# Rows scattered by expert during the attention, and one body per expert picked by its number of tokens

## The chip, the cores and the metric

One core of one Trainium2 chip. The time is the device time in microseconds of one execution, the median of the runs shown. The engines are named as in the profile: PE is TensorE (PEld its weight loads), DVE is VectorE, ACT is ScalarE, POOL is GpSimd, SP is SyncE. A "q" after an engine's name means its sequencer, the part that loads registers, waits for semaphores and branches. [...]

## What is computed

Chunked attention over 4 batches, 8 heads and 768 positions of 64 values, with 8 memory positions; its output, read as 3072 tokens of 512 values, goes through a mixture of 8 experts. Each token goes to one expert only:

```python
logits = x @ w_gate                      # 3072 x 512 by 512 x 8
expert_idx = np.argmax(logits, axis=1)
gate_w = softmax(logits)[own expert]
h = np.maximum(x_sorted[lo:hi] @ w1[e], 0.0)     # 512 x 1024
y_sorted[lo:hi] = h @ w2[e]                      # 1024 x 512
out = gate_w[:, None] * y                        # back in token order
```

All of it is fp32. The inputs are made with a fixed seed; worked through the reference, they give the 8 experts 529, 195, 426, 381, 565, 320, 162 and 494 tokens.

## The kernel before

`ordinary` does all the work; `general`, behind a test at the end (L890, L891), is a slower form for extreme inputs and is skipped here.

Attention. The loop at L726 goes over 32 blocks of 96 queries, and the order of the instructions is the order in which they are written. In iteration i it loads later blocks on SP's queue, transposes q of block i+2 (`turn_q`), computes `scores(i)` (L593, exponentials on ACT at L606), the values of heads 0 to 3 of block i-1 (`values`, L619, normalised on DVE at L622 and L623), transposes the rows of block i-2 (`turn_xb`, L633), the values of heads 4 to 7 of block i-1, transposes k of block i+3 (`turn_k`) and computes the gate's `logits(i-3)` (L645). These logits go into the last columns of the PSUM bank that `values(i-1, 1)` has filled, so they come after the DVE has read that bank (L623). The rows of a block, x, go to `x_dram` in token order by one DMA from POOL's queue (L626). After each batch of 8 blocks `route` picks the expert of each token and its place among that expert's tokens, in steps that the loop runs one by one; POOL adds up the counts per expert (`seen`, L678), PE turns them into ranks (`rk`, L680 and L681), and DVE writes for each block a 96 x 128 matrix `row_of` (L697).

Between the stages (L767 to L806) the counts are rounded up to tiles of 128 tokens, an expert is found for each of NS = 31 tiles, and a matrix product over the 32 blocks (L798, 64 matmul instructions) gives for each slot of each tile its token and its gate.

Experts. Each of the 31 tiles (L874) loads the w1 and w2 of its expert (2 MB each, SP, L815 and L817, two tiles ahead, address from a register), gathers its 128 rows from `x_dram` by an indirect DMA on POOL (L819), transposes them (`turn_xs`, L830, copied by DVE), computes the first layer (L842: 32 products of 128 x 128 by 128 x 128, each two matmul instructions, so 64), the second (L859: 8 products of 128 x 128 by 128 x 512, so 16 instructions), multiplies by the gate on ACT (L861) and scatters the rows to the output by an indirect DMA on POOL (L862).

Of the kernel before, what the change touches and what calls it, by code (L numbers as in the profile page):

```python
# [67 lines left out]
NV, NQ = 6, 4  # L68

# [25 lines left out]
def _consts():  # L95
# [4 lines left out]
    c["iota"] = np.broadcast_to(p, (128, 128))  # L100
    c["slot"] = np.broadcast_to(128 * np.arange(NS), (128, NS))
# [385 lines left out]
def ordinary(ctx, tc, q, k, v, mem_k, mem_v, moe_w_gate, moe_w1, moe_w2, out, good):  # L487
# [22 lines left out]
    x_dram = dpool.tile([N, DM], F32, name="x_dram")  # L510
# [6 lines left out]
    def const(name):  # L517
# [3 lines left out]
    ident, tri, iota, slot0, rev, token, mask = (  # L521
        const(n) for n in ("ident", "tri", "iota", "slot", "rev", "token", "mask")
# [19 lines left out]
    gate = cpool.tile([QB, NB], F32, name="gate")  # L542
    tile0 = cpool.tile([QB, NB], F32, name="tile0")
    row_of = cpool.tile([QB, NB, 128], F32, name="row_of")
# [65 lines left out]
    def values(i, g):  # L610
        s = st[i]
        if g == 0:
            s["x"] = apool.tile([QB, H, D], F32, name="x", bufs=3)

        bank = ps_o.tile([QB, 512], F32, tag="o", name="o")
# [7 lines left out]
        nc.vector.tensor_tensor(s["x"][:, 4 * g : 4 * g + 4], o[:, :, 0:D], bc(inv, 2, D), op=OP.mult)  # L623
        if g == 1:
            s["x"] = s["x"].rearrange("p h d -> p (h d)")
            nc.gpsimd.dma_start(x_dram[QB * i : QB * i + QB], s["x"])  # L626
        return bank[:, 4 * (D + 1) :]

# [10 lines left out]
    def logits(i, room):  # L639
# [3 lines left out]
        ps = room[:, 0:E]  # L643
        for c in range(DM // 128):
            mm(ps, lhsT=s["xT"][:, c], rhs=wg[:, c], start=c == 0, stop=c == DM // 128 - 1)  # L645
        nc.vector.tensor_copy(lgs[b][:, t], ps)


    def small(shape, name, dt=F32):
        return rpool.tile(shape, dt, name=name)  # L650

    def route(b):
# [17 lines left out]
        yield 1  # L670
        total = small([QB, NQB], "total")
        nc.vector.reduce_sum(total, l, axis=AX_X)
        nc.vector.tensor_scalar(total, total, 1e-9, None, op0=OP.add)
        nc.vector.reciprocal(gate[:, sl], total)
        yield 1

        for t in range(t0, t0 + NQB):
            nc.gpsimd.tensor_tensor(seen[:, t + 1], seen[:, t], onehot[:, t], op=OP.add)  # L678
# [3 lines left out]
        yield 1  # L682
        own = small([QB, NQB, E], "own")
        nc.vector.tensor_tensor(own, rk, oh, op=OP.mult)
        rank = small([QB, NQB], "rank")
        nc.vector.reduce_sum(rank, own, axis=AX_X)
        yield 1
        ri = small([QB, 3, NQB], "ri", I32)
        nc.vector.tensor_copy(ri[:, 0], rank)
        nc.vector.tensor_scalar(ri[:, 1], ri[:, 0], 127, None, op0=OP.bitwise_and)  # L690
        nc.vector.tensor_scalar(ri[:, 2], ri[:, 0], 0x1F80, None, op0=OP.bitwise_and)
        nc.vector.tensor_copy(tile0[:, sl], ri[:, 2])
        low = small([QB, NQB], "low")
        nc.vector.tensor_copy(low, ri[:, 1])
        yield 1
        for t in range(NQB):
            nc.vector.tensor_scalar(  # L697
                row_of[:, t0 + t], iota[0:QB], low[:, t : t + 1], None, op0=OP.is_equal
            )
            if t % 3 == 2:  # L700
                yield 1

# [11 lines left out]
    with tc.manual_schedule():  # L714
        for i in range(3):
            load_k(i)
            load_q(i)
            if i < 2:
                load_v(i)
# [6 lines left out]
        for i in range(NB + 3):  # L726
# [4 lines left out]
            need(i, scores)  # L731
            if 0 <= i - 1 < NB:
                values(i - 1, 0)
            need(i - 2, turn_xb)
            if 0 <= i - 1 < NB:
                room = values(i - 1, 1)
            else:
                room = ps_o.tile([QB, 512], F32, tag="o", name="o")
            need(i + 3, turn_k)
            if 0 <= i - 3 < NB:  # L740
                logits(i - 3, room)
                if (i - 3) % NQB == NQB - 1:
                    work.append(route((i - 3) // NQB))
            routing()
        while work:
            routing()

# [8 lines left out]
    nc.vector.tensor_scalar(good, okp[0:1], float(QB * 2 * NB * H), None, op0=OP.is_equal)  # L756

    actx.close()
    spool = ctx.enter_context(tc.tile_pool(name="spool", bufs=1))
    mpool = ctx.enter_context(tc.tile_pool(name="mpool", bufs=2))  # L760
    ps_s = ctx.enter_context(tc.tile_pool(name="ps_s2", bufs=2, space=PSUM))
    ps_t = ctx.enter_context(tc.tile_pool(name="ps_t2", bufs=3, space=PSUM))
    ps_o = ctx.enter_context(tc.tile_pool(name="ps_o2", bufs=2, space=PSUM))
    ps_r = ctx.enter_context(tc.tile_pool(name="ps_r2", bufs=1, space=PSUM))


    cnt = ps_r.tile([128, E], F32, tag="r", name="cnt")  # L767
    mm(cnt, lhsT=ones[0:QB], rhs=seen[:, NB], start=True, stop=True)
    ci = cpool.tile([128, 2, E], I32, name="ci")
    nc.vector.tensor_scalar(ci[:, 0], cnt, 127.0, None, op0=OP.add)  # L770
    nc.vector.tensor_scalar(ci[:, 1], ci[:, 0], 0x1F80, None, op0=OP.bitwise_and)
    size = cpool.tile([128, E], F32, name="size")
    nc.vector.tensor_copy(size, ci[:, 1])
    end = cpool.tile([128, E], F32, name="end")
    nc.vector.tensor_tensor_scan(end, ones[:, 0:E], size, 0.0, op0=OP.mult, op1=OP.add)
# [145 lines left out]
```

## Time and profile before

| what | us |
|---|---|
| median of 3 runs | 692.93 (691.35 to 693.66) |
| the profiled execution, time | 695.51 |
| its span in the trace | 693.7 |
| PE busy | 628.4 (91%) |
| first layer, L842, 1984 instructions | 228.2 |
| second layer, L859, 496 instructions | 218.0 |
| DVE, ACT, POOL busy | 124.3, 122.8, 89.4 |

The page shows three stages. For the first 190 us, the attention, PE is at nine tenths in most slices and the granted clock near full. Then come some 40 us in which PE is at five to nine tenths, DVE hands over to POOL and back, and the clock stands at half. From 230 us to the end PE is full at full clock while DVE, ACT and POOL are at one tenth, and the DMA engines are at 80 to 90% with the weights of the 31 tiles. The last 15 us hold no matmul. A view by stretch and the timeline of single tiles carry most of what follows; a sum of busy times over the span would mix the stages.

### The profile page before, as it was taken

How to read it: one execution, taken by the hardware profiler on the slowest of the kernel's cores; microseconds unless marked ns; L12 is line 12 of the kernel's file. 1: busy time of each engine (PE TensorE's matmuls, PEld its weight loads, DVE VectorE, ACT ScalarE, POOL GpSimd, SP SyncE). 2: the span in 40 equal slices, each digit the busy share in tenths (PEclk: the TensorE clock that was granted, in tenths of full speed). 3: DMA queues.
4: the chain of work that ended last, by engine and by line, in shares of the span. 5: the costliest groups of instructions: out<-in, count | busy, mean ns of one | idle time of the engine just before them, and what ended most of it. 6: DMA issues, size and time to landing. Idle time of an engine off the chain costs nothing. (4 is left out here: it accounts for less than half of the span.)

```text
span 693.7 us, 10193 instructions
## 1 busy us (share of the span) xinstructions
PE 628.4 (91%) x4096; PEld 500.6 (72%) x4096; DVE 124.3 (18%) x376; ACT 122.8 (18%) x259; POOL 89.4 (13%) x142
## 2 busy tenths in 40 slices
PE   3899899898727899999999999999999999999991
PEld 3798799798727767776677766777667776677760
DVE  1334444344360100010000100001000010000100
ACT  2445445354200001100011000110001100011000
POOL 1011100101121111111111111111111111110000
PEclk9999999899755799999999999999999999999997
DMA  9999968762129498989989899899898988988800
GB/s 153 158 196 204 203 136 186 160 139 61 36 80 385 151 339 302 323 318 335 335 304 326 324 335 337 304 325 334 332 336 301 331 312 329 343 306 309 297 3 3
DMA packets 143305, 173.26 MB, mean 250 GB/s; under 512 B 90446, under 2 KB 90574, under 8 KB 143248
## 3 DMA queue, kind: packets, MB, share of 16 engines
q1 hardware_dynamic: 135568, 151.54, 70.3%
q0 software_dynamic: 7008, 20.72, 8.4%
q8 instruction: 35, 0.57, 0.3%
q10 hardware_dynamic: 672, 0.25, 0.2%
q14 instruction: 22, 0.18, 0.1%
HBM read 159.90 MB, written 14.42 MB: 251 GB/s over the span
## 5 line engine op out<-in xcount | busy, mean ns | idle before, releaser
L842 PEld LDWEIGHTS ph<-xsT,w 128*128 128x128 f32 x1984 | 227.9, 193 | 14.5 <-issue 14.3
L842 PE MATMUL ph<-xsT,w 128*128 128x128 f32 x1984 | 228.2, 276 | 0.0
L859 PE MATMUL py<-w,h 128*128 128x512 f32 x496 | 218.0, 592 | 0.0
L859 PEld LDWEIGHTS py<-w,h 128*128 128x128 f32 x496 | 91.8, 190 | 103.8 <-issue 103.8
L851 DVE TENSOR_SCALAR h<-ph 128x512 f32<-128x512 f32 x31 | 21.4, 691 | 403.1 <-issue 381.7
L861 ACT ACTIVATE y<-py,gates 128x512 f32<-128x512 f32 x31 | 21.3, 687 | 317.9 <-PE py L859 308.0
L862 POOL DMA_INDIRECT out_dram<-y,dst x31 | 31.5, 1016 | 242.1 <-ACT y L861 242.1
L619 PE MATMUL o<-v,ex 128*96 128x65 f32 x512 | 54.4, 251 | 0.0
L619 PEld LDWEIGHTS o<-v,ex 128*96 128x96 f32 x512 | 53.4, 172 | 0.1
L593 PE MATMUL sc<-qT,kT 128*128 128x192 f32 x256 | 52.6, 353 | 0.0
L819 POOL DMA_INDIRECT xs<-x_dram,src x31 | 30.2, 974 | 170.0 <-PE txs L830 148.7
L593 PEld LDWEIGHTS sc<-qT,kT 128*128 128x128 f32 x256 | 45.5, 208 | 0.0
L576 ACT COPY qT<-tq 64x384 f32<-64x384 f32 x64 | 30.2, 472 | 69.1 <-PE tq L574 68.7
L606 ACT ACTIVATE ex<-sc,cst 128x256 f32<-128x256 f32 x96 | 38.5, 471 | 21.1 <-PE sc L593 21.1
L853 ACT ACTIVATE h<-ph 128x512 f32<-128x512 f32 x31 | 18.5, 597 | 125.8 <-PE ph L842 125.8
L645 PE MATMUL o<-wg,xT 128*96 128x8 f32 x256 | 28.5, 238 | 12.3 <-DVE x L623 12.2
L645 PEld LDWEIGHTS o<-wg,xT 128*96 128x96 f32 x256 | 25.9, 175 | 18.0 <-DVE x L623 16.1
L626 POOL DMA_DIRECT2D x_dram<-x x32 | 16.6, 520 | 162.9 <-DVE x L623 162.9
L584 PE MATMUL tk<-cst,kn 104*128 104x104 f32 x128 | 18.1, 267 | 10.4 <-DMA kn<-in_k_dram 10.3
L623 DVE TENSOR_TENSOR x<-o,inv_all 96x256 f32<-96x256 f32 x64 | 26.9, 420 | 2.2
L622 DVE RECIPROCAL inv_all<-o 96x4 f32<-96x4 f32 x64 | 11.4, 179 | 84.1 <-PE o L619 84.0
L830 PE MATMUL txs<-cst,xs 128*128 128x128 f32 x124 | 19.5, 283 | 6.9 <-DMA xs<-x_dram,src 6.9
(71 smaller groups left out, 232.2 us busy)
## 6 DMA issues: line engine op xcount, KB each, us to landing
w<-in_moe_w_dram SPq DMA_DIRECT2D x62, 2048.0 KB
kn<-in_k_dram SPq DMA_DIRECT2D x64, 96.0 KB
qn<-in_q_dram SPq DMA_DIRECT2D x32, 192.0 KB
x_dram<-x POOLq DMA_DIRECT2D x32, 192.0 KB, 3.6
v<-in_v_dram SPq DMA_DIRECT2D x24, 128.0 KB
v<-in_v_dram SPq DMA_DIRECT2D x24, 112.0 KB
v<-in_v_dram SPq DMA_DIRECT2D x8, 144.0 KB
v<-in_v_dram SPq DMA_DIRECT2D x8, 96.0 KB
```

What stands on the lines that cost most here:

```text
L576: nc.scalar.copy(qT[D * x : D * x + D, :, x], tq[D * x : D * x + D])
L593: mm(o.rearrange("p (x t) -> p x t", x=2), lhsT=turned[b][:, a, w0 : w0 + WIN], rhs=s["qT"][:, a], start=True, stop=True,)
L606: nc.scalar.activation(ex4[:, :, :, sl], sc4[:, :, :, sl], AF.Exp, bias=mask[:, 3 * x + g : 3 * x + g + 1], scale=D**-0.5)
L619: mm(o[:, j], lhsT=s["ex"][:, h], rhs=s["v"][:, h], start=True, stop=True)
L623: nc.vector.tensor_tensor(s["x"][:, 4 * g : 4 * g + 4], o[:, :, 0:D], bc(inv, 2, D), op=OP.mult)
L645: mm(ps, lhsT=s["xT"][:, c], rhs=wg[:, c], start=c == 0, stop=c == DM // 128 - 1)
L819: nc.gpsimd.indirect_dma_start(out=s["x"], out_offset=None, in_=x_dram, in_offset=bass.IndirectOffsetOnAxis(ap=src[:, a : a + 1], axis=0),)
L842: mm(ph[:, f], lhsT=s["w1"][:, c, c0 : c0 + 128], rhs=s["xT"][:, c], start=c == 0, stop=c == DM // 128 - 1,)
L851: nc.vector.tensor_scalar(o, ph, 0.0, None, op0=OP.max)
L859: mm(py, lhsT=s["h"][:, f], rhs=s["w2"][:, f], start=f == 0, stop=f == F // 128 - 1)
L861: nc.scalar.activation(y, py, AF.Copy, scale=gates[:, a : a + 1])
L862: nc.gpsimd.indirect_dma_start(out=out, out_offset=bass.IndirectOffsetOnAxis(ap=dst[:, a : a + 1], axis=0), in_=y, in_offset=None, bounds_ ...
```

## The change

In the attention, `logits(i-3)` comes before `values(i-1, 1)` and writes the end of the same bank first; its copy follows the DVE's normalisation. The first loads are in another order (q of block 1 ahead of v of block 0, q of block 2 ahead of v of block 1). x is written into one of two tiles `xr` for a whole batch, 528 columns wide, whose columns 512 and 513 take the token's number and its gate. `x_dram` has room for 1024 rows for each expert, and `route` ends with 8 indirect DMAs on POOL that scatter the rows of the 8 blocks straight to their expert's part. `row_of` and its steps, the DMA of x in token order and the whole matrix product between the stages are gone. The counts start from `ebase` (1024 e), so that a rank is a row in `x_dram` at once; the additions to `seen` stand two steps earlier than the product that reads them.

Then the loop is over 8 experts. The weights of each are loaded once, the first two without waiting for the routing. Up to 8 indirect gathers fetch the rows of an expert (rows beyond its count are out of bounds and left out); they wait for all 32 scatters. `tc.Switch` jumps, on PE, ACT, DVE and POOL, into one of 26 bodies, written for 0, 128, 160 ... 768, 832 ... 1024 tokens; SP stays outside of it. In a body the first layer runs over parts of 128 to 384 columns, the second over groups of up to 128 tokens, the copies go to ACT and DVE in turn, and the first two transposes of the next expert stand ahead of the last group's second layer.

```diff
-    x_dram = dpool.tile([N, DM], F32, name="x_dram")
+    x_dram = dpool.tile([E * XC, DX], I32, name="x_dram")
...
+WIDTHS = [0] + list(range(128, 769, 32)) + list(range(832, XC + 1, 64))
+CAP = 384
+def parts(n):
+    out, o = [], 0
+    while o < n:
+        r = n - o
+        w = r if r <= 256 or (r <= CAP and o > 0) else 128 if r <= CAP else 256
+        out.append((o, w))
+        o += w
+    return out
...
-        for i in range(3):
+        for i in range(2):
             load_k(i)
             load_q(i)
-            if i < 2:
-                load_v(i)
+        load_v(0)
+        load_k(2)
+        load_q(2)
+        load_v(1)
...
+            banks = [ps_o.tile([QB, 512], F32, tag="o", name="o") for _ in range(2)]
             if 0 <= i - 1 < NB:
-                values(i - 1, 0)
+                values(i - 1, 0, banks[0])
             need(i - 2, turn_xb)
+            late = logits(i - 3, banks[1]) if 0 <= i - 3 < NB else None
             if 0 <= i - 1 < NB:
-                room = values(i - 1, 1)
+                values(i - 1, 1, banks[1])
+            if late:
+                nc.vector.tensor_copy(*late)
...
+        for t in range(t0, t0 + NQB):
+            nc.gpsimd.tensor_tensor(seen[:, t + 1], seen[:, t], onehot[:, t], op=OP.add)
...
+        nc.vector.tensor_copy(dest[:, sl], row)
         for t in range(NQB):
-            nc.vector.tensor_scalar(
-                row_of[:, t0 + t], iota[0:QB], low[:, t : t + 1], None, op0=OP.is_equal
+            i = nc.gpsimd.indirect_dma_start(
+                out=x_dram,
+                out_offset=bass.IndirectOffsetOnAxis(ap=dest[:, t0 + t : t0 + t + 1], axis=0),
+                in_=xr[:, t].bitcast(I32),
...
-    for t in range(NB):
-        mm(who, lhsT=row_of[:, t], rhs=ent[:, t], start=t == 0, stop=t == NB - 1)
...
+    xes = [mpool.tile([128, NG, DX], F32, name=f"xe{i}", bufs=1) for i in range(2)]
+    for t in xes:
+        nc.gpsimd.memset(t, 0.0)
...
+    def expert(e, n):
+        todo = list(range(2, -(-n // 128)))
+        ps = parts(n)
+        for k, (o, w) in enumerate(ps):
+            h = mpool.tile([128, F // 128, CAP], F32, name="h")
+            need = -(-(ps[k + 1][0] + ps[k + 1][1]) // 128) if k + 1 < len(ps) else 0
+            for f in range(F // 128):
+                first_layer(e, h, o, w, f)
+                if f % 2 and todo and todo[0] < need:
+                    turn_x(e, todo.pop(0))
+            for j in range(0, w, 128):
+                if k + 1 == len(ps) and j + 128 >= w and e + 1 < E:
+                    turn_x(e + 1, 0)
+                    turn_x(e + 1, 1)
+                second_layer(e, h, o, j, min(128, w - j))
...
+        fetch_w(0)
+        fetch_w(1)
+        fetch_x(0)
+        fetch_x(1)
+        turn_x(0, 0)
+        turn_x(0, 1)
+        for e in range(E):
+            targets(e)
...
+            index = {
+                eng.engine: eng.value_load(case[0:1, 0, e : e + 1], min_val=0, max_val=len(WIDTHS) - 1)
+                for eng in engines
+            }
+            for a in tc.Switch(index, len(WIDTHS)):
+                expert(e, WIDTHS[a])
+            if e + 2 < E:
+                fetch_w(e + 2)
+                fetch_x(e + 2)
```

## Rows read from the trace of the kernel before

**Rows 1.** Busy time by stretch (windows view), core 0; columns in its first line.
```profile
core 0: us, PE busy (x) PEld busy (x) DVE busy (x) ACT busy (x) POOL busy (x), PEclk, DMA share, GB/s
26.00:177.00 151.00, 136.88 (x1261) 131.00 (x1261) 62.10 (x224) 72.63 (x175) 18.06 (x45) 0.96 0.79 158
193.00:230.00 37.00, 17.98 (x81) 17.12 (x82) 11.26 (x51) 0.26 (x1) 8.10 (x13) 0.50 0.66 249
230.00:679.00 449.00, 448.61 (x2596) 329.65 (x2595) 39.43 (x61) 39.42 (x62) 56.89 (x58) 1.00 0.83 302
```

**Rows 2.** Timeline of PE, last two tiles: start, us, engine, line, operation, count.
```profile
657.13 0.60 PE L830 MATMUL txs<-cst,xs 128*128 128x128 f32 x4
657.57 7.03 PE L859 MATMUL py<-w,h 128*128 128x512 f32 x16
664.44 7.31 PE L842 MATMUL ph<-xsT,w 128*128 128x128 f32 x64
671.58 7.03 PE L859 MATMUL py<-w,h 128*128 128x512 f32 x16
```

**Rows 3.** Timeline of PE, the first tile's first layer.
```profile
229.74 8.94 PE L842 MATMUL ph<-xsT,w 128*128 128x128 f32 x64
```

**Rows 4.** Sequencer instructions of L890 and L891: ns min/median/max, first and last start.
```profile
L890 PEldq TENSOR_LOAD <-good x1: 490/490/490, 672.6 to 672.6; - x1
...
L891 SPq EVENT_SEMAPHORE  x9: 17/17/17, 655.5 to 659.3; - x9
L891 SPq COMPARE_BRANCH  x1: 53/53/53, 650.6 to 650.6; - x1
L891 PEldq COMPARE_BRANCH  x1: 3785/3785/3785, 673.2 to 673.2; - x1
L891 PEldq EVENT_SEMAPHORE  x1: 51/51/51, 678.7 to 678.7; - x1
L891 ACTq COMPARE_BRANCH  x1: 50/50/50, 679.3 to 679.3; - x1
L891 ACTq EVENT_SEMAPHORE  x1: 17/17/17, 681.8 to 681.8; - x1
```

**Rows 5.** Waits, 26 to 177 us: us in total, times, longest.
```profile
PEld o L645 <- DVE x L623: 15.2, 27, 0.9
PE o L645 <- DVE x L623: 10.7, 27, 0.8
PE rk L681 <- POOL seen L678: 3.3, 2, 1.7
```

**Rows 6.** Timeline of the attention, PE, and its last DVE copy.
```profile
25.64 2.78 PE L593 MATMUL sc<-qT,kT 128*128 128x192 f32 x8
...
86.47 0.58 PE L681 MATMUL rk<-seen,ones 96*96 96x64 f32 x2 [1.71 <-POOL seen L678]
87.49 2.58 PE L593 MATMUL sc<-qT,kT 128*128 128x192 f32 x8
...
176.90 1.55 PE L593 MATMUL sc<-qT,kT 128*128 128x192 f32 x8
...
192.58 0.16 DVE L646 COPY lg<-o 96x8 f32<-96x8 f32 x1 [0.49 <-PE o L645]
```

**Rows 7.** Timeline of POOL after the attention.
```profile
195.60 2.12 POOL L678 TENSOR_TENSOR seen<-seen,onehot 96x8 f32<-96x8 f32 x8 [6.90 <-DVE lg L668]
...
222.82 0.98 POOL L819 DMA_INDIRECT xs<-x_dram,src  x1 [0.30 <-issue]
```

**Rows 8.** Memsets on POOL, by source line: ns min/median/max.
```profile
L532 POOL MEMSET qT<- x4: 411/411/413, 0.7 to 1.8; 64x384 f32 x4
...
L536 POOL MEMSET v<- x6: 117/131/131, 2.3 to 2.5; 128x8 f32 x6
```

**Rows 9.** DMA of tile out_dram (output scatters): issue to landing.
```profile
DMA to landing us min/median/max: 2.1/7.4/8.4
```

**Rows 10.** DMA of tile xs (gathers): issue to landing.
```profile
DMA to landing us min/median/max: 3.2/7.1/8.6
```

More of the change, by code (lines that the diff above doesn't have):

```diff
@@ L637, in ordinary, with logits @@
     lgs = {}
-    def logits(i, room):
+    def logits(i, bank):
         s, (b, t) = st[i], divmod(i, NQB)
@@ L670, in route @@
         yield 1
+        xr = xrs[b % 2]
         total = small([QB, NQB], "total")
@@ L768, in ordinary @@
[L768 to L775, printed above, removed]
@@ new lines, in ordinary, with fetch_x @@
+    nc.vector.tensor_tensor(rowf, rowf, there, op=OP.mult)
+    rows = cpool.tile([128, E, NG], I32, name="rows")
+    nc.vector.tensor_scalar(rows, rowf, float(E * XC), None, op0=OP.add)
+    therei = cpool.tile([128, E, NG], I32, name="therei")
+    nc.vector.tensor_copy(therei, there)
+    xes = [mpool.tile([128, NG, DX], F32, name=f"xe{i}", bufs=1) for i in range(2)]
+    for t in xes:
+        nc.gpsimd.memset(t, 0.0)
+    def fetch_x(e):
+        s = ms[e]
+        s["x"] = xes[e % 2]
+        for g in range(NG):
+            i = nc.gpsimd.indirect_dma_start(
+                out=s["x"][:, g].bitcast(I32),
+                out_offset=None,
+                in_=x_dram,
+                in_offset=bass.IndirectOffsetOnAxis(ap=rows[:, e, g : g + 1], axis=0),
+                bounds_check=E * XC - 1,
+                oob_is_err=False,
+            )
+            for j in scatters:
+                tc.add_manual_dep(
+                    i.ins, j, mybir.DependencyInfo(mybir.DependencyClass.Sync, mybir.DependencyReason.DATA)
+                )
@@ new lines, in targets, with move @@
+    def targets(e):
+        s = ms[e]
+        s["dst"] = mpool.tile([128, NG], I32, name="dst")
+        nc.vector.memset(s["dst"], SKIP)
+        nc.vector.copy_predicated(s["dst"], therei[:, e], s["x"][:, :, DM].bitcast(I32))
+    def move(out, in_, j, relu=False, scale=None):
+        if j % 2:
+            if relu:
+                nc.vector.tensor_scalar(out, in_, 0.0, None, op0=OP.max)
+            elif scale is not None:
+                nc.vector.tensor_scalar(out, in_, scale, None, op0=OP.mult)
+            else:
+                nc.vector.tensor_copy(out, in_)
+        elif scale is not None:
+            nc.scalar.activation(out, in_, AF.Copy, scale=scale)
+        else:
+            nc.scalar.activation(out, in_, AF.Relu if relu else AF.Copy)
@@ new lines, in turn_x, with first_layer @@
+    def turn_x(e, g):
+        s = ms[e]
+        tx = ps_x.tile([128, DM // 128, 128], F32, tag="x", name="txs")
+        for c in range(DM // 128):
+            turn(tx[:, c], s["x"][:, g, 128 * c : 128 * c + 128], ident)
+        move(s["xT"][:, :, 128 * g : 128 * g + 128], tx, g)
+    def first_layer(e, h, o, w, f):
+        s = ms[e]
+        ph = ps_h.tile([128, CAP], F32, tag="h", name="ph")
+        for c in range(DM // 128):
+            mm(
+                ph[:, 0:w],
+                lhsT=s["w1"][:, c, 128 * f : 128 * f + 128],
+                rhs=s["xT"][:, c, o : o + w],
+                start=c == 0,
+                stop=c == DM // 128 - 1,
+            )
+        move(h[:, f, 0:w], ph[:, 0:w], f, relu=True)
```

209 lines of the change are left out of this document (81 added, 128 removed).

## The prediction

> **What bounds the kernel now.** I read the view by stretch first [rows 1], then the timeline of single tiles [rows 2, 3], the waits of the attention [rows 5, 6], the stretch between the stages [rows 6, 7], and last the sequencers' instructions at the end [rows 4]. The reader is to see three kernels in one. From 26 to 177 us PE is busy 136.9 of 151 us: the attention is bound by PE, with some waits in it. From 193 to 230 us PE works 18 of 37 us at half clock: here a chain of small steps sets the time. From 230 to 679 us PE is busy 448.6 of 449 us at clock 1.00, with DVE, ACT and POOL below 13% each, so only fewer or cheaper matmul columns shorten that stage, and any idle time put into it lengthens the whole. The tail from the end of the last matmul (671.58 + 7.03 = 678.6 [rows 2]) to 693.7 is 15.1 us.
>
> **The attention.** From the scores of block 2 (25.64) to those of block 31 (176.90) it is 151.26 us [rows 6]. The logits move ahead of the second values, so PE no longer stands until DVE has read the bank: 10.7 us of waits on PE and 15.2 on PEld [rows 5]; I take 13, between the two, as weight loads and products overlap. The copy of the logits moves behind DVE's normalisation; the next one that wants its bank is 4 us later, so that costs nothing (0.2 us a block if that cover is gone). `seen` is added two steps before `rk` reads it, which removes 3.3 us [rows 5]. After such a wait the clock falls: the scores after the wait at 86.47 took 2.58 us, at full level 1.55 [rows 6]. The mean clock of 0.96 [rows 1] means 12 us at the lower level, up to 6 us lost; 4.5 of it comes back, the rest belongs to the start. So 151.3 - 13 - 3.3 - 4.5 = 130.5, and block 31 is reached at 156.1. From there to the last copy of logits it was 192.74 - 176.90 = 15.8; less one `rk` wait (1.65, half of 3.3), four logits waits of 0.5 and about 1.5 for the lower level, 10.7. The last logits are there at 166.8 instead of 192.7.
> What is late next: the loads. The DMA share was 0.79 [rows 1]; the same bytes in 130.5 us make 0.92, so PE stays the bound, with up to 5 us against me. The new order of loads changes which of the first blocks waits, not the bytes up to block 4: nothing. The 32 scatters on POOL replace 32 plain DMAs: about 1.28 us each by the gathers' spacing [rows 7], on an engine busy 18 of 151 us [rows 1]; 24 of them lie beside the attention and cost nothing; without that cover it would be 31 us. The dropped `row_of` work was on DVE, which is at 41%: worth nothing but 1.6 us at the very end, counted below. The first 8 MB of weights, until now behind the routing, follow the last load on SP and land beside the attention.
>
> **Between the stages.** From the last logits to the first layer it was 229.74 - 192.74 = 37.0 us. Now: five DVE operations to the one-hot 1.4; additions on POOL 2.1 [rows 7]; `rk` and three DVE operations 1.5; the last 8 scatters 8 x 1.28 = 10.2; two memsets of 4224 columns on POOL, 3.3 us each at the slope of [rows 8] (0.745 ns a column), 6.6; the second gather 1.3 later and landed in 3.2, the least of [rows 10], as the weights are in by then; transposes 0.45. That is 26.7. The gathers stand on POOL behind a wait for all 32 scatters; behind them stand POOL's own jump and the output scatters, and PE's first transposes wait for them; the landing lies beside the memsets. Bounds: the memsets may run earlier (0), the landing may be 8.6 [rows 10]: -7 to +5. Then PE's first jump, 5.2 (below): 31.9. The first layer starts at 198.7 instead of 229.7.
>
> **The experts' work.** The counts give the bodies 544, 224, 448, 384, 576, 320, 192 and 512: 3200 columns in 14 parts, 28 groups of the second layer. One instruction of 128 columns takes 7.14 us / 64 = 111.6 ns (664.44 to 671.58), one of 512 takes 6.87 / 16 = 429.4 (657.57 to 664.44) [rows 2]; the line through both is 0.828 ns a column and 5.7 ns. First layer: 64 x (3200 x 0.828 + 14 x 5.7) = 174.6 us, where it was 31 x 7.14 = 221. Second: 28 x 6.87 = 192.4 (213). Transposes: 27 x 0.44 = 11.9. At the start the lower clock costs 8.94 - 7.31 = 1.6 [rows 3]. Together 380.5 instead of 448.9. Weights come once, 8 x 4 MB where it was 31 x 4: the DMA was not the bound, so worth nothing by itself. Copies on ACT and DVE lie beside PE.
>
> **The jumps.** This is the price of the change, and only the test at the end of the old kernel shows one [rows 4]. Three things are to be seen there. A taken branch costs time: 3.785 us on PE; on ACT 681.8 - 679.3 = 2.5 from the branch to the next instruction; on SP 655.5 - 650.6 = 4.9, while weights were still moving. The sequencer of PE loads its register at 672.6, 6.0 us ahead of the last matmul's end, so a jump can be hidden behind queued work. But the instruction after it stands at 678.7, right behind that end: at the join each engine brings its semaphores up to those of the path not taken, and waits for its own work first. A body chosen out of 26 is shorter than the longest one, so I expect that wait at the end of every body. Behind it on PE stand the exit, the load of the index, the jump and the whole next body; nobody else can give PE work. Per jump: end and exit 0.3, load 0.6 (672.6 to 673.2), arithmetic 0.6 by its few instructions, the branch, 0.2 to the first product. For the branch the bounds are 2.5 (ACT) and 7.4 (PE's 3.785 times SP's 4.9 over 2.5, as SP releases the next weights at just that moment); I take 5.0, nearer to PE's own row. That is 6.7 us of idle PE (5.2 ahead of the first body: no exit, and PE's own 3.785, as no weights are moving). Then the lower clock: 1.6 [rows 3] to 3; I take 2.0. Seven jumps between experts: 7 x 8.7 = 61 us. Bounds 7 x 5.8 = 41 and 7 x 12.1 = 85. ACT and DVE jump at the same time and are wanted only when the first product of a body is done, 1.7 us later. POOL waits at a body's end for its scatters to land (7.4 at the median, [rows 9]), then issues up to 8 gathers, 10 us, which land in 7 [rows 10]: about 26 us after the body's end, where the shortest next one (192 columns) wants its rows after some 25. So POOL is just in time, and hidden for all longer ones.
> [...]
>
> **The tail.** It was 15.1 us. The output's last scatter now has to land (2.1 at least, [rows 9]) before POOL leaves its body and comes to the old test: 17.5.
>
> **The sum.** 198.7 + 380.5 + 61 + 17.5 = 657.7 us of span, against 693.7. What lies around the span (695.51 - 693.7) adds 1.8, and the profiled run was 2.6 above the median of the three: 656.9, I say 657. By the bounds above: 657 - 2 - 7 - 20 = 628 and 657 + 5 + 5 + 24 = 691.
>
> **Rivals.** (1) The jump is hidden: the body ends without a wait for PE's own work, the queue covers load and branch, and some 0.6 us remain per jump. For it: the 6.0 us. Against it: 678.7. Time 657 - 61 + 4 = 600. (2) The exit of a body is a taken branch as well and pays like the entry, another 5.0: 657 + 35 = 692, no change. For it: the old exit, if such, is a plain branch over code. [...] (3) Slower: exit and entry both pay the price under load, 7.4 each, as SP starts 4 MB of weights at every body's end; 1.5 + 14.8 + 0.2 + 3.0 = 19.5 per jump, 7 x 19.5 = 136 instead of 61, time 732. It decides from 13.8 us per jump on (8.7 and the gain of 36 over 7). For it: SP's 4.9 beside ACT's 2.5. Against: PE's jump comes within 2 us of the body's end, when little of the weights is queued. That the slow `general` runs, or a body for more tokens than there are, is excluded by the counts: the largest is 565 of 1024.
>
> **How the numbers follow.** Forecast 0.63, rival 1 0.12, rival 2 0.14, rival 3 0.11. The range takes the forecast's bounds, a little below for half-hidden jumps, and rival 2: 622 to 696; it leaves out rivals 1 and 3. A measurement of this kernel tells some 0.3% from no change. Forecast and rival 1 are faster; of rival 2, 0.08 is faster, 0.04 within 0.3% and 0.02 slower; rival 3 is slower. So 0.83, 0.04, 0.13.
>
> **What would show it.** In the new trace: the gap before logits <- DVE gone and the last logits near 167; scatters on POOL some 10 us, the first layer near 199; first-layer instructions of 256 columns spaced by 217 ns; in each of seven places a gap of PE of about 7 us that holds a wait for PE's own semaphore, a load and a branch, and a clock of 0.5 behind it. Wrong it would be if the gap is under 2 us or over 12, if PE waits for rows that POOL fetched late, or if the attention is held by its loads.

## The result and the profile after

The changed kernel took 643.4 us (641.55 to 646.45, 4 runs) where the kernel before took 693.29 (691.35 to 693.75, 4 runs): a ratio of 0.929 (0.9243 to 0.9336). The forecast was 657 with a range of 622 to 696. The profiled execution took 641.84 us, with a span of 640.0. Its sum, term by term, beside the forecast:

| term, us of span | predicted | measured | difference |
|---|---|---|---|
| last logits copied at | 166.8 | 161.2 | -5.6 |
| from there to the first layer | 31.9 | 40.0 | +8.1 |
| the experts' work | 380.5 | 380.5 | 0 |
| seven jumps between experts | 61 | 46.8 | -14.2 |
| tail | 17.5 | 11.6 | -5.9 |
| span | 657.7 | 640.0 | -17.7 |

The measured 380.5 is the length of the experts' stage in the kernel without jumps, shown below; the 46.8 are what the stage of the changed kernel is longer than that.

The windows view of the changed kernel, with the stretches that answer to [rows 1]: 

```profile
core 0: us, PE busy (x) PEld busy (x) DVE busy (x) ACT busy (x) POOL busy (x), PEclk, DMA share, GB/s
26.00:152.00 126.00, 124.11 (x1252) 123.33 (x1251) 55.06 (x200) 71.71 (x173) 19.57 (x40) 1.00 1.05 199
160.00:201.00 41.00, 5.23 (x26) 3.93 (x25) 5.53 (x36) 0.95 (x3) 30.00 (x33) 0.53 0.44 141
201.00:628.40 427.40, 394.71 (x1448) 257.30 (x1448) 39.62 (x93) 39.18 (x87) 82.30 (x83) 0.96 0.27 89
```

Three things are to be seen. In the attention PE is busy 124.1 of 126 us at clock 1.00 (the granted clock as a share of full speed), where it had waited 14 us of 151 at 0.96. The stretch between the stages still has PE at 5 of 41 us and at half clock. The experts' stage takes 427.4 us at 0.96, of which PE is busy 394.7, where it took 449 at 1.00, and its DMA share is 0.27. The first layer starts at 201.15 instead of 229.74 [rows 3], the last matmul ends at 628.4 instead of 678.6 [rows 2].

The groups of the page that stand where the two layers stood (busy, mean ns; then the idle time just before them):

```profile
L880 PE MATMUL ph<-xsT,w 128*128 128x256 f32 (+5 forms) x896 | 193.2, 378 | 37.5 <-issue 14.6
...
L893 PE MATMUL py<-w,h 128*128 128x512 f32 (+3 forms) x448 | 195.9, 593 | 0.0
```

896 first-layer instructions take 193.2 us (1984 took 228.2), 448 of the second take 195.9 (496 took 218.0). Ahead of the first layer PE stood idle for 37.5 us, and ahead of the second not at all: whatever idle time the experts' stage still has stands at the start of a body; the lower clock behind it comes on top.

### The profile page after: what moved, and what is told of

Same layout as the page of the kernel before. It is cut to its first block, busy times and chain, and to the rows that moved or that the text cites. A ratio compares the mean times of both kernels' runs of the same rounds, so it can differ in the third digit from the quotient of the medians.

```text
span 640.0 us, 7913 instructions
## 1 busy us (share of the span) xinstructions
PE 547.1 (85%) x2884; PEld 405.9 (63%) x2884; DVE 111.7 (17%) x368; ACT 122.7 (19%) x285; POOL 137.4 (21%) x176
## 5 line engine op out<-in xcount | busy, mean ns | idle before, releaser
L880 PE MATMUL ph<-xsT,w 128*128 128x256 f32 (+5 forms) x896 | 193.2, 378 | 37.5 <-issue 14.6
L880 PEld LDWEIGHTS ph<-xsT,w 128*128 128x128 f32 x896 | 166.4, 206 | 66.8 <-issue 26.3
L893 PE MATMUL py<-w,h 128*128 128x512 f32 (+3 forms) x448 | 195.9, 593 | 0.0
L893 PEld LDWEIGHTS py<-w,h 128*128 128x128 f32 (+3 forms) x448 | 79.2, 179 | 103.0 <-issue 102.4
L835 POOL DMA_INDIRECT xe<-x_dram,rows x64 | 64.3, 1004 | 57.4 <-issue 30.3
L867 ACT ACTIVATE h<-ph 128x256 f32<-128x256 f32 (+5 forms) x56 | 20.0, 361 | 221.8 <-PE ph L880 176.4
L859 DVE TENSOR_SCALAR h<-ph 128x256 f32<-128x256 f32 (+5 forms) x56 | 22.0, 396 | 206.3 <-PE ph L880 165.9
L707 POOL DMA_INDIRECT x_dram<-xr,dest x32 | 29.6, 924 | 39.7 <-DVE dest L704 21.0
L873 PE MATMUL txs<-cst,xe 128*128 128x128 f32 x112 | 16.7, 284 | 23.8 <-DMA xe<-x_dram,rows 23.8
L642 DVE TENSOR_TENSOR xr<-o,inv_all 96x256 f32<-96x256 f32 x64 | 26.9, 421 | 2.2
```

The source lines that it names most:

```text
L642: nc.vector.tensor_tensor(x[:, 4 * g : 4 * g + 4], o[:, :, 0:D], bc(inv, 2, D), op=OP.mult)
L707: i = nc.gpsimd.indirect_dma_start(out=x_dram, out_offset=bass.IndirectOffsetOnAxis(ap=dest[:, t0 + t : t0 + t + 1], axis=0), in_=xr[:, t] ...
L835: i = nc.gpsimd.indirect_dma_start(out=s["x"][:, g].bitcast(I32), out_offset=None, in_=x_dram, in_offset=bass.IndirectOffsetOnAxis(ap=rows ...
L859: nc.vector.tensor_scalar(out, in_, 0.0, None, op0=OP.max)
L873: turn(tx[:, c], s["x"][:, g, 128 * c : 128 * c + 128], ident)
L880: mm(ph[:, 0:w], lhsT=s["w1"][:, c, 128 * f : 128 * f + 128], rhs=s["xT"][:, c, o : o + w], start=c == 0, stop=c == DM // 128 - 1,)
```

## The experiments

Each ratio is against the kernel before, run on the same chip.

### The attention by itself

The kernel before, with only the two edits inside the attention: the logits ahead of the second values, and the additions to `seen` two steps earlier.

```diff
             need(i - 2, turn_xb)
+            late = logits(i - 3, banks[1]) if 0 <= i - 3 < NB else None
             if 0 <= i - 1 < NB:
-                room = values(i - 1, 1)
+                values(i - 1, 1, banks[1])
+            if late:
+                nc.vector.tensor_copy(*late)
...
+        for t in range(t0, t0 + NQB):
+            nc.gpsimd.tensor_tensor(seen[:, t + 1], seen[:, t], onehot[:, t], op=OP.add)
+
         nc.vector.tensor_tensor(l, l, bc(top, 2, E), op=OP.subtract)
```

> The kernel before with two edits of the change alone: the logits ahead of the second values in the same bank, and the additions to seen two steps earlier. Nothing else. If these two carry the gain of the attention, the period of a block falls from 4.915 to about 4.34 us as in the changed kernel, the last copy of logits comes near 163 instead of 192.7 us, and the time falls by 26 to 31 us, to about 665. The rival, that the new order of loads, the x written by scatters or the dropped row_of work carry it, leaves the period above 4.7 and the time above 682.

Measured: 668.19 us (666.95 to 668.61), ratio 0.9642 (0.9606 to 0.9679). So 25 of the 50 us come from the order of the instructions in the attention and have nothing to do with the experts. The first layer of this kernel starts at 203.2 us, that of the changed kernel at 201.15. The matrix product over the 32 blocks is gone, and the chain that replaces it is no shorter: from the last logits to the first layer it is 37.1 us here and 40.0 in the changed kernel. The attention of the changed kernel ends 5 us earlier (161.2 against 166.15); which of its other edits gives these 5, no run separates. The other 26 us of span (666.4 - 640.0) are these 2, 20.6 of the experts' stage (447.9 against 427.3) and 3.7 of the tail.

### The logits without the earlier additions

As above, with the additions to `seen` left where they were.

> The kernel before with the logits ahead of the second values, and nothing else: the additions to seen stay right before the product that reads them. Theory: this order gives the shorter period of a block (0.57 us by 29 blocks, 16 to 17 us), and the additions the rest of the 25 us of the attention run (two or three waits of 1.6 us and the lower clock behind them): 693 - 17 = 676. Rival: the waits for seen are taken up by other slack, and nearly all of the 25 us is there: 669.

Measured: 685.91 us (682.38 to 686.31), ratio 0.9865 (0.9836 to 0.9895). Both expectations were too good. PE's timeline around the first batch's ranks, the columns as in [rows 6]:

```profile
82.00 0.38 PE L679 MATMUL rk<-seen,ones 96*96 96x64 f32 x2 [2.98 <-DMA v<-in_v_dram]
...
82.55 2.47 PE L593 MATMUL sc<-qT,kT 128*128 128x192 f32 x8
```

PE now comes to the ranks earlier, while POOL's additions are not earlier by as much: the wait for `seen` is 2.98 us where it was 1.71 [rows 6] (the releaser written there is only the last of several). Behind it two iterations run at the lower clock (2.47 and 2.77 us for scores that take 1.49), and the three from the scores at 74.69 to those at 95.70 take 7.86, 7.14 and 6.01 us instead of 4.35 each: 8.0 us lost. In the kernel before, the same place lost 3.8. The second place like it loses 8.7 us in place of 5.2, and a third wait is 3.23 instead of 1.55. That gives back 4.2 + 3.5 + 1.7 = 9 of the 17 us that the order gains in 29 periods (4.93 us each before, 4.35 now), and 8 are left. With the additions moved as well, the place costs 1.1 us in the changed kernel. The one edit is worth 8 us by itself and the two 25, so the price of either depends on the other; the additions alone were not run.

### The eight bodies without a jump

The bodies of the eight counts of this input written one after the other; the choice by the counts is left out.

```diff
-            for a in tc.Switch(index, len(WIDTHS)):
-                expert(e, WIDTHS[a])
+            expert(e, (544, 224, 448, 384, 576, 320, 192, 512)[e])
```

> The changed kernel with the eight bodies written out one after the other for these inputs' counts (544, 224, 448, 384, 576, 320, 192, 512) and no jump. It leaves out the choice by the counts. Theory: the jumps cost the idle stretches of PE behind the eight bodies' entries (4.9 at the first, 32.5 us in the other seven) and some 10 us of lower clock after them: 643 - 48 = 595. A rival, that these stretches come from rows or weights that arrive late, leaves the time above 630.

Measured: 590.48 us (587.37 to 591.25), ratio 0.8511 (0.8471 to 0.8551). The window from the first to the last matmul of the experts, columns as above:

```profile
200.20:580.70 380.50, 380.47 (x1448) 246.33 (x1448) 39.40 (x93) 39.79 (x87) 85.43 (x86) 1.00 0.28 97
```

PE is never idle in it and the clock stays at 1.00; its length is the predicted 380.5 to the decimal. So all jumps together cost 643.4 - 590.5 = 52.9 us by the medians. By the spans (640.0 and 589.3) it is 50.7: 46.8 in the experts' stage (427.3 - 380.5), 0.95 ahead of the first layer and 3.0 in the tail. The 0.95 is less than the first entry costs: the gap before the first layer falls from 4.91 to 0.83 us, but in this run the attention ended 2 us later and the scatters landed 1.3 later, so that the first transposes stand at 196.92 in place of 193.74. Of the 46.8, 32.5 are idle time of PE (the rows below without the 4.9 of the first entry); the other 14.3 are matmuls at the lower clock. Of these, 1.1 stand behind the first entry (the first 16 matmuls take 6.52 us in place of 5.40), which leaves 1.9 for each of seven jumps.

The idle time of PE in the experts' stage of the changed kernel, from the waits view (total, times, longest):

```profile
PE ph L880 <- issue: 14.6, 6, 4.9
PE ph L880 <- ACT h L867: 12.3, 4, 4.2
PE ph L880 <- DVE h L859: 8.0, 2, 5.7
PE ph L880 <- ACT y L865: 1.4, 1, 1.4
PE ph L880 <- DVE y L861: 1.1, 1, 1.1
```

### Where the time of a jump goes

This needs no experiment, only one jump of the changed kernel, that between the third and the fourth expert, in its timeline:

```profile
355.60 0.37 SPq L810 DMA_DIRECT2D w<-in_moe_w_dram  x1
...
356.38 7.08 PE L893 MATMUL py<-w,h 128*64 128x512 f32 x16
...
363.55 0.74 DVE L861 TENSOR_SCALAR y<-py,xe 64x512 f32<-64x512 f32 x1 [6.38 <-PE py L893]
...
365.36 2.02 PE L880 MATMUL ph<-xsT,w 128*128 128x128 f32 x16 [1.90 <-issue]
...
366.66 0.28 ACT L867 ACTIVATE h<-ph 128x128 f32<-128x128 f32 x1 [9.88 <-PE ph L880]
...
374.96 0.49 DVE L859 TENSOR_SCALAR h<-ph 128x128 f32<-128x128 f32 x2 [7.47 <-issue]
...
375.31 2.08 PE L880 MATMUL ph<-xsT,w 128*128 128x128 f32 x8 [5.70 <-DVE h L859]
```

and in the sequencers' rows of the same stretch, first those that load the index of the body (L939), then the branches (x2: the exit from the old body is the first, the entry to the new one the last start):

```profile
L939 PEldq TENSOR_LOAD <-case x1: 324/324/324, 356.8 to 356.8; - x1
...
L939 DVEq TENSOR_LOAD <-case x1: 318/318/318, 367.3 to 367.3; - x1
```

```profile
L981 ACTq COMPARE_BRANCH  x2: 43/45/47, 356.1 to 362.0; - x2
L981 PEldq COMPARE_BRANCH  x2: 335/3744/7152, 356.4 to 357.8; - x2
...
L981 DVEq COMPARE_BRANCH  x2: 48/57/66, 363.6 to 368.2; - x2
```

PE's exit stands at 356.4 and took 0.34 us, its load follows at 356.8, its entry at 357.8, and that took 7.15 us. All this time the array works: its last 16 instructions run from 356.38 to 363.46. PE's sequencer is 7 us ahead, loads and jumps meanwhile, and only 1.90 us of its jump are seen. The engine that has the last y isn't ahead, here DVE: it does that y at 363.55, and only then come its exit (363.6), its load (367.3), its entry (368.2), and the first h of the new body at 374.96, 11.5 us after the end of the old one. PE has three PSUM banks for `ph`; with the second not emptied it stands from 369.60 to 375.31. ACT, which had no part in the last y, left at 356.1 and copies its first h at 366.66, right behind PE's first product. So a jump has two gaps: a first of 1.1 to 2.2 us (12.2 us in seven) and a second of 2.0 to 5.7 (20.3 us in six; the last jump has none). The first stands behind PE's own branch in six jumps, where that ends 1.1 to 1.8 us after the old body's last matmul; in the last jump it ended 1.5 us before, and the 1.1 us are a wait for the last y. The second stands behind the jump of the engine that had the last y.

### Weights that are not loaded

Experts 2 to 7 compute with the weights of experts 0 and 1, which stay where they are; 24 MB are not loaded.

```diff
-                fetch_w(e + 2)
+                ms[e + 2]["w1"], ms[e + 2]["w2"] = ms[e]["w1"], ms[e]["w2"]
                 fetch_x(e + 2)
```

> The changed kernel without the loads of the weights of experts 2 to 7: they use those of experts 0 and 1, so part of the input is left out. All jumps stay. Theory: the branch fetches code through the same DMA engines as the weights and is slow beside them: PE's entry branch falls from 6.6 to 7.5 us to about 4.2 in all places, ACT's and DVE's from 6 to about 3, the first idle stretch at a body's start goes, the second shrinks to about 1; 20 to 28 us faster than the changed kernel, near 619. Rival, a fixed cost of control flow and semaphores: the branch keeps 7 us and the time 643.

Measured: 616.72 us (616.22 to 618.25), ratio 0.8901 (0.8868 to 0.8934), as expected. PE's branches at the entries and exits, first in the changed kernel, then in this one (ns, least, median and largest):

```profile
L981 PEldq COMPARE_BRANCH  x14: 311/2222/7496, 263.2 to 565.5; - x14
```

```profile
L981 PEldq COMPARE_BRANCH  x15: 311/351/4001, 264.3 to 596.8; - x15
```

The largest falls from 7.5 to 4.0 us. The row counts exits (0.3 us) with entries; in the changed kernel the last entry, when no weights are left to load, took 4.1. On ACT and DVE the time from a branch to the next instruction falls from some 6 to 2.5 and 2.8. That code moves can be seen in the DMA queues of the page (packets, MB, share of 16 engines), here one of the two queues for instructions, first in the changed kernel, then in the one without jumps:

```profile
q14 instruction: 111, 0.91, 0.5%
```

```profile
q14 instruction: 20, 0.16, 0.1%
```

With the other one (46 packets against 25) the kernel with jumps moves 1.1 MB of code more, over the DMA engines that also carry the weights. In the 7.2 us of PE's entry in the jump above (357.8 to 365.0) the queues brought:

```profile
q1 hardware_dynamic: 476, 1.85, 72.8%
...
q14 instruction: 4, 0.03, 2.0%
q8 instruction: 2, 0.03, 1.6%
```

That is six packets of code beside 1.85 MB of weights. For which engine a packet was, the trace doesn't tell. So I read these rows together: an engine that jumps waits for its code, and longer while weights move; whether the code stands in line behind them or shares the engines with them, no run shows. The price here is 4.0 to 4.3 us on PE, and 6.6 to 7.5 with weights under way.

### The same weights, a little later

The weights of experts 2 to 7 go out from POOL's queue, where they come behind POOL's own jump, just ahead of the gathers, instead of from SP as soon as their place is free. Nothing is left out.

```diff
+        q = nc.sync if e < 2 else nc.gpsimd
...
-        nc.sync.dma_start(s["w1"], moe_w1[e]
+        q.dma_start(s["w1"], moe_w1[e]
```

> The changed kernel with the weights of experts 2 to 7 loaded from POOL's queue, just ahead of the gathers of the same expert, and so some 7 to 9 us after the end of a body instead of 8 us before it. All is computed. Theory: the jumps of PE and ACT are over when the weights start to move and take 4 and 2.6 us instead of 7.3 and 6; the time comes near that of the run without those weights, 617 to 623. Rival: the weights then arrive too late, or hold up the gathers on POOL, and PE waits for them at the start or end of a body: above 640.

Measured: 619.19 us (618.77 to 622.68, 5 runs), ratio 0.8932 (0.8894 to 0.8969), as expected. PE's branches:

```profile
L982 PEldq COMPARE_BRANCH  x15: 311/351/4261, 264.8 to 597.7; - x15
```

They are nearly as short as without weights (4.26 us at most, 4.00 there), and no matmul waits for weights. Counted from the end of a body, w1 is asked for 14 us later than in the changed kernel and w2 7 us later (362.05 and 362.86 behind an end at 355.95, where it was 355.60 and 363.49 with the end at 363.46). So the 24 us are the price of moving code and weights at once: the same bytes a little later cost 2.5 us more than no bytes at all (619.19 and 616.72).

### The last y on the same engine

The last y of a body always goes to ACT, and of the first eight h of the next body DVE copies the first six.

```diff
-        move(h[:, f, 0:w], ph[:, 0:w], f, relu=True)
+        move(h[:, f, 0:w], ph[:, 0:w], by, relu=True)
...
-                first_layer(e, h, o, w, f)
+                first_layer(e, h, o, w, f, 1 if k == 0 and f < 6 else f)
...
-                second_layer(e, h, o, j, min(128, w - j))
+                last = k + 1 == len(ps) and j + 128 >= w
+                second_layer(e, h, o, j, min(128, w - j), 0 if last else (o + j) // 128)
```

> The changed kernel with two assignments changed: the last result of a body always goes to ACT, and the first six blocks of a body's first part are all emptied by DVE. Theory: the second idle stretch after a jump is the wait for whichever of ACT and DVE had the last result, since its exit, load and jump (2.6 + 0.9 + 6 us) begin only when PE has ended; with DVE free seven microseconds earlier and ACT not wanted at first, the second stretches (20.3 us in sum) and their share of the lower clock go and the first ones (12.2) stay: 643 - 22 = 621. Rival: both engines are late in any case, since their jumps are slow beside the weights, and the time stays above 637.

Measured: 619.03 us (614.97 to 620.67), ratio 0.8918 (0.8866 to 0.8971), as expected. Its first jump:

```profile
270.60 0.68 ACT L865 ACTIVATE y<-py,xe 32x512 f32<-32x512 f32 x1 [6.83 <-PE py L893]
...
272.01 4.21 PE L880 MATMUL ph<-xsT,w 128*128 128x224 f32 x21 [1.45 <-ACT y L865]
...
275.25 0.69 DVE L859 TENSOR_SCALAR h<-ph 128x224 f32<-128x224 f32 x2 [5.28 <-issue]
```

ACT has the last y at 270.60. DVE left the old body at 263.6, seven microseconds earlier, so that its entry stands at 270.75 and its first h at 275.25, in time for PE. The first gap stays (1.45); the second is gone here and shrinks from 20.3 to 7.4 us over the stage, all of it now a wait for DVE, whose jumps are still slow (4.5 us from entry to first h in this one). PE's branches take about as long as in the changed kernel (7.2 us at most, there 7.5). The second gap therefore is the lateness of the one engine that PE needs first.

### One more bank

`ps_h` has four banks in place of three.

> The changed kernel with four PSUM banks for the first layer's results instead of three. Theory: after a jump PE stops because ACT or DVE is not yet in its body to empty a bank, so one more bank lets PE do one more block of 128 hidden values (0.9 to 1.8 us) in each of seven places: 7 to 11 us faster, near 634. Rival, that PE stops for its own jump alone: 643.

Measured: 637.76 us (632.14 to 638.92), ratio 0.9187 (0.9129 to 0.9246). The direction is right, the size smaller than expected, and the interval touches that of the changed kernel. The second gaps became 3.8, 1.3, 5.1, 0.7, 4.1 and 4.1 us, 19.1 in place of 20.3: three of them shrank, by 0.6 to 1.6, and the last grew by 2.1. The stage is 5.9 us shorter (421.4), with 2.4 less idle time of PE; the other 3.5 are matmuls less at the lower clock. One bank, which holds a block of 0.9 to 1.7 us, doesn't bridge an engine that comes 11 us late.

### The memsets on another engine

```diff
     for t in xes:
-        nc.gpsimd.memset(t, 0.0)
+        nc.vector.memset(t, 0.0)
```

> The changed kernel with the two memsets of the experts' tiles on DVE instead of POOL. They stood 7.2 us on POOL between the landing of the scatters and the first gather. Theory: the first gather waits for the first of the two alone (some 3.5 to 4 us on DVE), so 3 to 4 us are gained, near 640; if the landing of the scatters were what the gathers wait for, nothing is gained.

Measured: 644.12 us (641.54 to 649.83), ratio 0.9311 (0.9244 to 0.9377): no difference that can be measured, against the expectation. Its timeline:

```profile
184.85 3.58 DVE L829 MEMSET xe<- 128x4224 f32 x1 [13.08 <-issue]
...
189.31 1.04 POOL L835 DMA_INDIRECT xe<-x_dram,rows  x1 [9.04 <-DVE xe L829]
...
199.70 5.53 PE L880 MATMUL ph<-xsT,w 128*128 128x256 f32 x14 [4.12 <-issue]
```

A memset takes as long on DVE (3.58 us) as on POOL (7.18 for two). It starts at 184.85, so it still comes behind the landing of the scatters, which in this run is 4.6 us after the last of them and was 2.7 in the changed kernel; that takes back part of what was expected. The first gather waits for it until 189.31, where it was 189.97. The first layer is 1.45 us earlier. To gain the 7 us, the memsets would have to come ahead of the landing, and that was not tried.

### The last counts on DVE

The additions to `seen` of the last batch on DVE, as POOL is still in the scatters of the batch before.

```diff
-            nc.gpsimd.tensor_tensor(seen[:, t + 1], seen[:, t], onehot[:, t], op=OP.add)
+            (nc.vector if b == B - 1 else nc.gpsimd).tensor_tensor(seen[:, t + 1], seen[:, t], onehot[:, t], op=OP.add)
```

> The changed kernel with the last batch's additions to seen on DVE instead of POOL. Theory: they waited 4.2 us on POOL behind the scatters of the batch before, and everything up to the first body waits for them: the wait of rk falls from 5.6 to about 1 us, the first layer starts at 196 to 197 instead of 201.2, and the time falls by 4 to 5 us, to 639. Rival: POOL is busy with those scatters anyway and the scatters of the last batch start no earlier: 643.

Measured: 664.5 us (660.85 to 668.9, 6 runs), ratio 0.9578 (0.9542 to 0.9614): 21 us slower than the changed kernel instead of 4 faster. The wait for `seen` did fall from 5.63 to 0.96 us. But two stalls have come into the attention, far ahead of the place that was edited. The first of them:

```profile
86.68 0.22 PE L637 MATMUL o<-v,ex 128*96 128x65 f32 x1 [0.95 <-issue]
...
90.95 0.18 DVE L640 RECIPROCAL inv_all<-o 96x4 f32<-96x4 f32 x1 [9.26 <-remote]
...
92.20 0.90 PE L647 MATMUL tx<-cst,xr 96*128 96x96 f32 x4 [5.31 <-DVE kT L605]
```

PE's last product before it runs at 86.68, after two gaps for which no releaser is shown (0.20 and 0.95); DVE, which waits for the products, goes on at 90.95 after 9.26 us, ACT at 91.06, and PE itself only at 92.20. The iteration took 13.4 us instead of 4.35; a second like it, near 140 us, took 12.65. Both lie beside eight scatters on POOL. The same scatters cause none in the changed kernel, and the kernel of the next section has this very edit and no such stall. What holds the products back stays open. Two further kernels that were to settle it, this edit with the memsets and the kernel of the next section without it, have no time. So what the edit is worth rests on the traces alone: from the first product of the last ranks (L698) to the first layer it is 34.9 us here and 38.6 in the changed kernel, 3.7 less.

### Together

The late engine, the later weights, four banks, the memsets and the last counts on DVE.

> The four edits together: last result on ACT and first blocks on DVE, four banks, weights from POOL's queue after the body, the memsets on DVE; and the last batch's additions to seen on DVE, which waited 4.2 us on POOL behind the scatters of the batch before. If the edits are additive as far as their stretches differ: 590 (no jump at all) plus some 1 to 2 us per jump and 5 at the first, less 8 between the stages: 595 to 602.

Measured: 602.52 us (601.9 to 604.6), ratio 0.8699 (0.8658 to 0.874), just above what was expected, and 41 us better than the changed kernel. Its experts' stage and the waits of PE in it:

```profile
195.40:586.20 390.80, 382.75 (x1448) 246.67 (x1448) 46.66 (x114) 33.74 (x66) 93.49 (x95) 0.99 0.27 97
```

```profile
PE ph L881 <- issue: 10.4, 8, 4.6
```

```profile
L881 PEldq EVENT_SEMAPHORE  x16: 51/51/2591, 195.2 to 527.7; - x16
```

The seven gaps are 0.81 to 0.87 us each (10.4 with the 4.6 of the first entry), one group of rows comes 1.82 late, and the clock is 0.99. These gaps are no longer the jump. The last row (ns, least, median, largest) is PE's sequencer waiting for a semaphore ahead of the first product of a body: at each of the seven jumps PE has its code by then and stands there for 2.0 to 2.6 us, until ACT has copied the last y (0.68 us). PE's own jump is hidden wholly. Against the changed kernel the first layer starts 5.7 us earlier (195.42), the stage is 36.5 shorter (390.8), and the tail 3.2 longer. The first of these holds the 4.3 us of the last counts: rank products at 164.47 in place of 168.75.

## Why the prediction was right, and where it wasn't

**The experts' work** held to the decimal: the line through the two durations of [rows 2] carries over to parts of 128 to 320 columns, and 380.5 us stands in the kernel without jumps. The decimal is luck: the sum counted 27 groups of transposes where 26 stand in the stage (0.4 us less), and the lower clock at the start cost 1.8 us (5.40 for 3.62) where I had 1.6.

**The jumps** were the price, as forecast, and 46.8 us of the 61; but they are not made as I said. The step that failed is "I expect that wait at the end of every body". It rested on one row, the test at the end [rows 4], where PE's next instruction came right behind its own last matmul. The changed kernel still has that at its very end, but PE leaves a body with 7 us of matmuls queued. Rival 1 was right about this: the queue covers load and branch. At the exit of the jump above (356.40) the first of the last 16 pairs of weight load and matmul had just begun in the array; their products run from 356.38 to 363.46. What the test at the end waits for was my reading of the semaphore rows of L891; why it joins with a wait and the choice of a body without, no run shows.

Rival 1's time, 600, still was wrong, for a sentence of mine that I took as harmless: "ACT and DVE jump at the same time and are wanted only when the first product of a body is done". They don't jump at the same time. The engine with the last y starts its jump when PE's work ends, and has exit and entry ahead of it. That is rival 2's price, on another engine than rival 2 had it: an exit cost ACT, DVE and POOL 2.5 to 3.0 us without weights under way and up to 6 with them, PE 0.3. The experiment with the last y on ACT shows it: with two assignments of copies changed, the second gaps fall from 20.3 to 7.4 us and the time by 24. The 0.6 us that rival 1 left for a jump came to 0.8 with all edits together, but as a wait for the last y.

**The size of a branch** lay between the bounds: 6.6 to 7.5 us for PE beside the weights, the upper bound of 7.4 rather than the 5.0 taken, and 4.1 without weights, near the row of 3.785 [rows 4]. I argued that "PE's jump comes within 2 us of the body's end, when little of the weights is queued". This is wrong as well: SP asks for w1 of the next but one expert as soon as the last group but one of the second layer is done, some 8 us ahead of the body's end (355.60 against 363.46 in the timeline above), and PE's entry comes 1.8 to 2.3 us after that. The upper price on PE was mostly hidden by its queue; on ACT and DVE it was not. Of the 47 us of idle time that I had put behind PE's own jump 12 came, and 20 came from the other engines, which I had put at nothing: the term is right to 14 us because two errors met from opposite sides, and that is luck. The branch's own record on ACT and DVE is only 43 to 66 ns in that jump, and on PE up to 7.5 us; what a jump costs is the time until the next instruction, 6.6 us for DVE's entry (368.2, next 374.8). The small terms around the branch (0.3, 0.6 and 0.2) were estimates without a row; in that jump PE's exit took 0.34 us, and from the end of its load to the branch it is 0.7, from the end of the branch to the first product 0.4. The lower clock after a jump, taken as 2.0 us between the 1.6 of [rows 3] and 3, came to 1.9.

**The attention** was mis-sized by 5.6 us, in the right direction. PE's timeline, from the scores of one block to the next:

```profile
99.94 1.49 PE L613 MATMUL sc<-qT,kT 128*128 128x192 f32 x8
...
101.92 0.50 PE L647 MATMUL tx<-cst,xr 96*128 96x96 f32 x4
102.26 0.77 PE L659 MATMUL o<-wg,xT 128*96 128x8 f32 x8
102.88 0.87 PE L637 MATMUL o<-v,ex 128*96 128x65 f32 x8
...
104.29 1.49 PE L613 MATMUL sc<-qT,kT 128*128 128x192 f32 x8
```

The logits (L659) follow the transposes without a gap, then come the second values. A period is 4.35 us where it was 4.93; from block 2 (24.38) to block 31 (151.88) it is 127.5 us where I had 130.5. The loads start 1.3 us better, and the last steps took 9.3 instead of 10.7. The loads came close to being what is late next: the DMA share is 1.05 in that stretch, more than the 0.92 worked out. But PE waits for them only 0.6 us in it, so PE still is the bound.

**Between the stages** I was 8.1 us too low. POOL's timeline and PE's:

```profile
165.90 0.92 POOL L707 DMA_INDIRECT x_dram<-xr,dest  x1 [0.30 <-issue]
166.83 2.14 POOL L684 TENSOR_TENSOR seen<-seen,onehot 96x8 f32<-96x8 f32 x8
170.49 0.92 POOL L707 DMA_INDIRECT x_dram<-xr,dest  x1 [1.52 <-DVE case L776]
...
179.05 0.92 POOL L707 DMA_INDIRECT x_dram<-xr,dest  x1 [0.30 <-issue]
182.63 7.18 POOL L829 MEMSET xe<- 128x4224 f32 x2 [2.66 <-DMA x_dram<-xr,dest]
189.97 1.05 POOL L835 DMA_INDIRECT xe<-x_dram,rows  x1 [0.15 <-POOL xe L829]
```

```profile
168.75 0.58 PE L699 MATMUL rk<-seen,ones 96*96 96x64 f32 x2 [5.63 <-POOL seen L684]
...
193.74 1.09 PE L873 MATMUL txs<-cst,xe 128*128 128x128 f32 x4 [23.51 <-DMA xe<-x_dram,rows]
...
201.15 4.18 PE L880 MATMUL ph<-xsT,w 128*128 128x256 f32 x9 [4.91 <-issue]
```

Three terms: the additions to `seen` stand on POOL behind the eight scatters of the batch before and so start at 166.83, 4.3 us late, a queue that I had moved them past without counting it; the memsets come behind the landing of the scatters (2.66 us of wait) and not beside it; and the transposes of the first expert, at half clock and one gather after the other, took 2.5 us where I had 0.45. The scatters themselves, 1.22 us apart, were priced well by the gathers [rows 7], as were the memsets by the slope of [rows 8] (7.2 for 6.6). The first entry took 4.3 us on PE and left a gap of 4.91 where I had 5.2.

**The tail** was 11.6 instead of 17.5. A row that I had not read for the sum goes with it, the last step of POOL's sequencer, in the kernel before and the changed one (ns, least, median, largest):

```profile
L916 POOLq DRAIN  x3: 40/107/7750, 685.1 to 693.4; - x3
```

```profile
L981 POOLq DRAIN  x3: 40/113/898, 638.3 to 639.8; - x3
```

The long one is 7.75 us in the kernel before and in that of the attention alone, 4.24 in the two kernels that load weights from POOL's queue, and 0.7 to 0.9 in six that have no plain DMA on that queue. The change took 32 such DMAs from it. That these cause the long end is only argued from this pattern; no run tests it alone.

**The rest.** The landing of the gathers was 2.2 us at the median and not 3.2, and POOL was in time for all experts, as said. Rival 3 was out: its price per jump, 19.5, is three times the 6.7 us (46.8 / 7) that was paid.

## What to carry to other kernels

In these runs the entry to a body chosen at run time cost each engine 2.5 to 4.3 us, and up to 7.5 with weights under way, and the engine that counted was the one that had the last work before it. So give the last work of a body and the first work of the next to different engines (24 us here), and start no large transfer just as the engines jump (24 us here). An engine with work queued ahead of it can hide its jump, as PE did with 7 us of matmuls. An edit that lets one engine arrive earlier at a wait can be worth little until what it waits for is earlier too (the logits alone 8 us, with the earlier additions 25), so cost such edits in pairs.

## What the runs showed of the hardware that was not expected

- A branch into a body of the choice took PE 4.1 and 4.3 us in the changed kernel where no weights were being loaded, and 6.6 to 7.5 while they were. On ACT, DVE and POOL it was 2.5 to 3.6 us from a branch to the next instruction, and mostly 4 to 6.6 beside the weights. PE's exit from a body took 0.3 us, the other engines' exits 2.5 to 6.1.
- PE's sequencer was 7 us ahead of the array at a body's end (356.40 against 363.46), 16 pairs of weight load and 512-column matmul; with the weights out of the way (all edits together) that hid PE's exit, load and entry wholly.
- The last step of POOL's sequencer took 0.7 to 0.9 us in six kernels without plain DMAs on its queue, and 4.24 or 7.75 in four with them.
- Two stalls, of 5 us of PE and 8 to 9 of ACT and DVE, in one kernel, beside eight indirect scatters; their cause is open.
